# A Fourier stage whose 64x64 products become 32x32 after one more round of sums on GpSimd

## The chip, the cores and the metric

One core of one Trainium2 chip runs the program. The metric is device time in microseconds (us) of one execution. Engines are called as in the profile: PE is TensorE, DVE VectorE, ACT ScalarE, POOL GpSimd, SP the engine that issues most DMAs.

## The reference

The inputs are 8 batches of 3008 rows by 256 channels. Each batch is transformed along its rows, mixed over channels in the frequency domain, clipped softly, transformed back, and put through a wide layer with a cosine.

```
X = rfft(x, axis=1)                      # 3008 = 64 * 47 rows
Yr = Xr @ w_r - Xi @ w_i + b_r
Yi = Xr @ w_i + Xi @ w_r + b_i
Y  = sign(Y) * max(|Y| - 0.01, 0)        # for Yr and Yi
y  = irfft(Yr + 1j * Yi, axis=1)         # 24064 rows of 256 in all
h  = y @ w_in                            # 256 -> 2048
out = (h * cos(h)) @ w_out               # 2048 -> 256
```

## The kernel before, in words

The row index is split into 64 times 47 (padded to 48). Stage A takes the 64-point transform, stage B the 47-point one (`forward`), the mixing (`combine`, `wmix`), the folding (`fold`) and the inverse 47-point transform (`spread`, matmuls into `pi`); stage C takes the inverse 64-point transform (into `pc`) and turns the result for the wide layer. The wide layer runs in steps, 16 steps for each of 6 column tiles of a batch, so 96 steps a batch: `moe_step` multiplies by `win` into `ph`, makes the cosine product `u` on ACT and DVE, rounds it to `gh` on ACT, and takes the rest `gl = u - gh`. `gl` is made on POOL for the even steps (`POOL_GL = (0, 2)`) and on DVE for the odd ones. `second` multiplies `gh` and `gl` by `wout` into `po`, three steps later (`SKEW = 3`).

The Fourier work of batch b+1 is written between the wide layer's steps of batch b by generators that give back costs (`pull`, `share`), and a scheduler fixes from that the order of instructions on each engine. Each engine then runs its own list strictly in order. On POOL the list mixes `gl` with the tile sums of stage A, the sums of `combine` (`both`, `Xl`), the folding (`st`, `odd`), and the issue of DMAs (`xt`, `fq`). So a late `gl` holds PE at the line of `second` that reads it, and whatever stands ahead of `gl` in POOL's list makes it late.

Stage A of batches 2 to 7 handles six tiles a batch, two at a time: three groups a batch, 18 in all. `load` issues the DMA of a tile `xt` (512 KB) from POOL's queue; two tiles are in flight. `fold` adds and subtracts the two mirrored halves on POOL (line 460 writes `xe`, line 461 overwrites part of `xt`). `burst_of` then lets PE multiply both tiles: eight products of 64x64 with 512 columns each (a product shows as two rows of the trace). A burst is issued as one piece where its inputs allow it. ACT copies the four PSUM banks out (line 499), SP stores them to `scr1`, and the loads of the tiles two further on are issued. The sums of a group follow its loads, and its burst comes some 40 us later. After a batch's third group the next batch's first two tiles are loaded and summed.

Of the kernel before, what the change touches and what calls it, by code (L numbers as in the profile page):

```python
# [86 lines left out]


def _constants():
    n1, s = np.arange(64), np.arange(32)  # L90
    ang = 2 * np.pi * (np.outer(n1, s) % 64) / 64
# [25 lines left out]
    for sl in range(1, 32):  # L117
        for k2 in range(47):
            sig[sl, k2] = 1 if crt[sl, k2] <= N // 2 else -1
# [61 lines left out]
def tile_body(ctx: ExitStack, tc, x, w_r, w_i, b_r, b_i, w_in, w_out,  # L181
# [26 lines left out]
    def load_constants():  # L208
        with nc.allow_non_contiguous_dma(reason="bias"):
            for r, bsrc in enumerate((b_r, b_i)):  # L210
                nc.gpsimd.dma_start(bb[:, r, :], bsrc.rearrange("(c p) -> p c", p=128))
        ws["sig"] = pool["pro"].tile([96, 32], F32, name="sig", bufs=1)
        nc.gpsimd.dma_start(ws["sig"], c_sig)
        nc.gpsimd.dma_start(fi[0], c_if)
        ws["minus"] = wk.tile([128, 64], F32, tag="xe", name="minus", bufs=2)
        nc.gpsimd.tensor_scalar(out=ws["minus"], in0=ff[:, 256:], scalar1=-1.0, scalar2=None, op0=ALU.mult)
# [169 lines left out]
    def stage_out(name):  # L386
        return wk.tile([128, 1024], F32, tag="ao", name=name, bufs=3)
# [52 lines left out]
    def stage_a(b):  # L440
        scr1[b] = dr.tile([2, 24, 32, 2, 256], F32, tag="scr1", name=f"scr1_{b}")
        ld, ev = {}, {}

        def load(c):
            if c < 6:
# [4 lines left out]
                if b == 2 and c < 2:  # L450
                    behind(ins, mark["pc"].ins, "first tile")

        def fold(c):
            with floor() if b == 2 else ExitStack():
                sums(c)

        def sums(c):
            ev[c] = wk.tile([128, 2, 256], F32, tag="xe", name="xe", bufs=2)
            lo, hi = ld[c][:, :, 0], ld[c][:, :, 1]
            nc.gpsimd.tensor_tensor(out=ev[c], in0=lo, in1=hi, op=ALU.add)  # L460
            nc.gpsimd.tensor_tensor(out=lo, in0=lo, in1=hi, op=ALU.subtract)

        def store(c, ao, after=None):
            for v in range(2):
                ins = nc.sync.dma_start(
                    scr1[b][v, 4 * c:4 * c + 4].rearrange("i s r d -> (s r) i d"),
                    ao[64 * v:64 * v + 64].rearrange("p (i d) -> p i d", i=4))
                if after is not None:
                    behind(ins, after.ins, "first tile")
# [7 lines left out]
        def burst_of(cs, banks=None, home=stage_out):  # L477
# [3 lines left out]
            p = {(c, h): ps2[2 * (c - cs[0]) + h] for c in cs for h in range(2)}  # L481
            if b == 1:
                ins = burst(1 if odd else 2, [((p[c, h][64 * v:64 * v + 64], (ws["minus"] if v * g else ff[:, 256:])[64 * h:64 * h + 64],
                            ld[c][64 * h:64 * h + 64, :, g]),
                           dict(start=g == 0, stop=g == 1, skip_group_check=True))
                          for c in cs for g in range(2) for h in range(2) for v in (1, 0)])
                if pro:
                    mark["fill"] = mark["pa"] = ins
            else:
                burst(len(ps2), [((p[c, h][64 * v:64 * v + 64], ff[64 * h:64 * h + 64, 256:320],  # L490
                                   (ld[c][64 * h:64 * h + 64, :, 0] if v else ev[c][64 * h:64 * h + 64])),
                                  dict(start=True, stop=True, skip_group_check=True))
                                 for c in cs for h in range(2) for v in (1, 0)])
            if banks:
                yield 0.0
            for c in cs:
# [9 lines left out]
                else:  # L506
                    store(c, ao)
                if b > 1:
                    del ld[c], ev[c]
                    load(c + 2)  # L510
            yield BURST

        def folds(j):
            for c in (2 * j, 2 * j + 1):
                fold(c)
                yield 0.5
# [14 lines left out]
        def begin():  # L531
            load(0)
            load(1)

        return SimpleNamespace(begin=begin, folds=folds, alone=alone, release=release, one=lambda *a: burst_of([a[0]], *a[1:]),
                               group=lambda j: burst_of([2 * j, 2 * j + 1]))


    def stage_b(b):
# [15 lines left out]
        def load(q):  # L555
            if b and q < 4:
# [4 lines left out]
                for h in range(4):  # L561
                    own = q == 0 and SLOT0[h] != SLOTS[h]
                    r0 = 64 * (h // 2) + 24 * (h % 2)
                    for (v, r), s0, s1 in ((SLOT0[h], 0, 1), (SLOTS[h], 1, 8)) if own else ((SLOTS[h], 0, 8),):
                        ins = nc.sync.dma_start(t[r0:r0 + 24, 256 * s0:256 * s1].rearrange("j (s d) -> j s d", d=256),
                                                scr1[b][v, :, 8 * q + s0:8 * q + s1, r])
                        loads.append(ins)
# [462 lines left out]
    COST = 4 * (6 * GROUP + 2 * TURN + 11.0 + MIXED + QUIET + 3 * READ + BURST + QUIET + 3 * READ + BURST)  # L1030
    A_COST = 3 * (1.0 + QUIET + 3 * READ + BURST)
    HEAD = 3 * (READ + BURST) + START + BT_WAIT + FIRST
# [98 lines left out]
```

## Time and profile before

| what | value |
|---|---|
| median of 3 runs | 2578.68 us (2576.16 to 2579.6) |
| the profiled execution, its own time | 2579.13 us |
| its span | 2577.1 us |
| PE busy | 2549.1 us, 99% of the span |
| DVE, ACT, POOL busy | 72%, 65%, 40% |
| mean granted clock of TensorE | 0.998 |

The span is from the first to the last instruction; about 2.0 us lie around it. A busy share is an average over stages; PE's 99% says that PE is hardly ever idle, and where it is idle must be read from the order in time.

### The profile page before, as it was taken

What the parts mean: (1) busy time and instruction counts of PE and PEld (TensorE: products, weight loads), DVE (VectorE), ACT (ScalarE), POOL (GpSimd) and SP (SyncE); (2) the same over time, 40 slices, a digit from 0 to 9 for tenths busy, and PEclk for the clock granted to TensorE, in tenths of its full rate; (3) what the DMA queues carried; (4) which work ended last, traced back from release to release, by engine and by line L of the source; (5) the groups of instructions that cost most, each with busy time, mean ns of one, the idle gap of its engine ahead of it and who ended that gap; (6) DMA issues with size and microseconds to landing.
All of it is one profiled execution on the core that took longest, in us unless ns stands there. A gap on an engine that the chain in (4) does not pass through costs nothing.

```text
span 2577.1 us, 42991 instructions
## 1 busy us (share of the span) xinstructions
PE 2549.1 (99%) x15961; PEld 2063.7 (80%) x15961; DVE 1850.8 (72%) x2909; ACT 1679.6 (65%) x3119; POOL 1026.6 (40%) x1002
## 2 busy tenths in 40 slices
PE   9999999999999999999999999999999999999999
PEld 7577777877788777887788777887788888888888
DVE  5887766777667776777767777677776777766665
ACT  5766666666666666666666666666676666666666
POOL 2135552555334453345623545245442444222222
PEclk9999999999999999999999999999999999999999
DMA  7545444444334443254423544345433244210000
GB/s 238 188 115 148 134 116 118 112 130 139 111 82 126 136 132 98 82 154 142 130 83 98 155 131 119 91 101 144 132 104 104 85 116 114 62 45 17 17 25 16
DMA packets 172954, 283.12 MB, mean 110 GB/s; under 512 B 15608, under 2 KB 114200, under 8 KB 169160
## 3 DMA queue, kind: packets, MB, share of 16 engines
q1 hardware_dynamic: 161896, 243.78, 33.6%
q0 software_dynamic: 10112, 35.53, 4.4%
q8 instruction: 126, 2.06, 0.3%
q10 hardware_dynamic: 736, 1.05, 0.1%
q14 instruction: 84, 0.69, 0.1%
HBM read 149.76 MB, written 130.55 MB: 109 GB/s over the span
## 4 chain that ended last, share of the span: by engine, by line
PE 85%; DVE 5%; DMA 3%; ACT 2%; issue 2%; POOL 2%; SPq 0%; ACTq 0%; DVEq 0%; POOLq 0%
PE ph L936 12%; PE po L918 12%; PE po L922 12%; PE ph L937 12%; PE ph L938 12%; PE po L919 12%; PE pw L676 2%; PE pw L678 2%; PE pw L677 2%; PE pc L383 1%; PE pb L383 1%; DVE u L950 1%; DMA xt<-in_dram 1%; DVE u L947 1%; PE pw L672 1%
## 5 line engine op out<-in xcount | busy, mean ns | idle before, releaser
L331 POOL TENSOR_TENSOR gl<-u,gh 128x512 fp32r<-128x512 f32 (+1 forms) x384 | 494.0, 1286 | 1079.9 <-ACT gh L951 913.9
L949 ACT ACTIVATE u<-u 128x512 f32<-128x512 f32 (+1 forms) x768 | 478.4, 623 | 348.0 <-DVE u L947 346.9
L947 DVE SCALAR_TENSOR_TENSOR u<-ph,u 128x512 f32<-128x512 f32 (+1 forms) x768 | 515.9, 673 | 258.4 <-ACT u L946 256.5
L950 DVE TENSOR_TENSOR u<-ph,u 128x512 f32<-128x512 f32 (+1 forms) x768 | 518.5, 676 | 252.7 <-ACT u L949 240.5
L946 ACT ACTIVATE u<-ph 128x512 int32<-128x512 f32 (+1 forms) x768 | 449.9, 587 | 256.1 <-PE ph L938 248.0
L918 PE MATMUL po<-gh,wout 128*128 128x512 f32 (+1 forms) x1536 | 598.9, 390 | 4.4 <-ACT gh L951 4.4
L936 PE MATMUL ph<-xTh,win 128*128 128x512 f32 (+1 forms) x1536 | 601.5, 392 | 0.2
L951 ACT CAST gh<-u 128x512 fp32r<-128x512 f32 (+1 forms) x768 | 467.6, 610 | 202.3 <-DVE u L950 198.3
L937 PE MATMUL ph<-xTl,win 128*128 128x512 f32 (+1 forms) x1536 | 594.5, 387 | 0.0
L938 PE MATMUL ph<-xTh,win 128*128 128x512 f32 (+1 forms) x1536 | 594.0, 387 | 0.0
L919 PE MATMUL po<-gh,wout 128*128 128x512 f32 (+1 forms) x1536 | 593.6, 386 | 0.0
L922 PE MATMUL po<-gl,wout 128*128 128x512 f32 (+1 forms) x1536 | 477.8, 388 | 5.2 <-POOL gl L331 5.2
L334 DVE TENSOR_TENSOR gl<-u,gh 128x512 fp32r<-128x512 f32 (+1 forms) x384 | 304.6, 793 | 76.1 <-ACT gh L951 68.1
L936 PEld LDWEIGHTS ph<-xTh,win 128*128 128x128 f32 x1536 | 288.5, 188 | 87.5 <-issue 19.0
L922 PEld LDWEIGHTS po<-gl,wout 128*128 128x128 f32 x1536 | 287.2, 188 | 71.9 <-POOL gl L331 9.6
L918 PEld LDWEIGHTS po<-gh,wout 128*128 128x128 f32 x1536 | 288.6, 188 | 66.1 <-ACT gh L951 7.6
L938 PEld LDWEIGHTS ph<-xTh,win 128*128 128x128 f32 x1536 | 288.8, 188 | 56.3
L919 PEld LDWEIGHTS po<-gh,wout 128*128 128x128 f32 x1536 | 288.8, 188 | 51.1 <-issue 0.4
L937 PEld LDWEIGHTS ph<-xTl,win 128*128 128x128 f32 x1536 | 288.8, 188 | 51.0
L676 PE MATMUL pw<-Xh,wf 128*128 128x384 f32 x336 | 114.3, 340 | 2.9 <-ACT Xh L613 2.9
L716 POOL TENSOR_TENSOR odd<-st 128x184 f32<-128x184 f32 (+1 forms) x112 | 66.7, 595 | 122.0 <-DVE st L693 119.4
L677 PE MATMUL pw<-Xh,wf 128*128 128x384 f32 x336 | 113.4, 338 | 0.0
(119 smaller groups left out, 2443.6 us busy)
## 6 DMA issues: line engine op xcount, KB each, us to landing
scrF<-at SPq DMA_DIRECT2D x28, 1024.0 KB
z<-scrF SPq DMA_DIRECT2D x112, 256.0 KB
scrT<-tr SPq DMA_DIRECT2D x56, 512.0 KB
y<-scrT SPq DMA_DIRECT2D x112, 256.0 KB
bt<-scr SPq DMA_DIRECT2D x94, 256.0 KB
scr<-bo SPq DMA_DIRECT2D x224, 96.0 KB
scr<-ao SPq DMA_DIRECT2D x80, 256.0 KB
out_dram<-ob SPq DMA_DIRECT2D x80, 256.0 KB
```

What stands on the lines that cost most here:

```text
L331: return nc.gpsimd.tensor_tensor(out=lo, in0=x, in1=hi.bitcast(F32), op=ALU.subtract)
L918: mm(po[e][:, :n], wo[0][:, 0, f, es], gh[:, :n], start=f == 0, stop=False)
L919: mm(po[e][:, :n], wo[0][:, 1, f, es], gh[:, :n], start=False, stop=False)
L922: mm(po[e][:, :n], wo[0][:, 0, f, es], gl[:, :n], start=False, stop=f == NFC - 1)
L936: mm(h, win[:, 0, c, fs], th[:, c, :n], start=c == 0, stop=False)
L937: mm(h, win[:, 0, c, fs], tl[:, c, :n], start=False, stop=False)
L938: ins = mm(h, win[:, 1, c, fs], th[:, c, :n], start=False, stop=c == 1)
L946: nc.scalar.activation(k[:, :n], h, AF.Identity, bias=0.25, scale=1.0 / TWO_PI)
L947: nc.vector.scalar_tensor_tensor(out=u[:, :n], in0=h, scalar=1.0 / TWO_PI, in1=k[:, :n], op0=ALU.mult, op1=ALU.subtract)
L949: nc.scalar.activation(u[:, :n], u[:, :n], AF.Sin, bias=HALF_PI, scale=TWO_PI)
L950: product = nc.vector.tensor_tensor(out=u[:, :n], in0=h, in1=u[:, :n], op=ALU.mult)
L951: step = [nc.scalar.copy(gh[:, :n], u[:, :n])]
```

## The change

For batches 2 to 7, POOL makes two rounds of sums instead of one. `halve` first adds and subtracts rows n and n+32 of a tile, which the host has laid side by side, into `xe` (now one buffer of twice the size). `fold` then adds and subtracts the mirrored halves from `xe` back into `xt`. The sums of rows need the even frequencies only, the differences the odd ones, so `octet` multiplies two tiles by sixteen products of 32x32, on sixteen parts of the array, in place of eight of 64x64. The outputs lie ordered by parity, and the constants, `scr1` and the loads from it follow that order. POOL has four sums for a tile where it had two (72 more in all); the number of bytes, of DMAs and of copies out of PSUM stays.

```
+        def halve(c):
+            with floor() if b == 2 else ExitStack():
+                t = wk.tile([128, 2, 2, 256], F32, tag="xe", name="xe", bufs=1)
+                ev[c] = t
+                one, two = ld[c][:, :, 0], ld[c][:, :, 1]
+                nc.gpsimd.tensor_tensor(out=t[:, 0], in0=one, in1=two, op=ALU.add)
+                nc.gpsimd.tensor_tensor(out=t[:, 1], in0=one, in1=two, op=ALU.subtract)
+
         def fold(c):
             with floor() if b == 2 else ExitStack():
-                sums(c)
-
-        def sums(c):
-            ev[c] = wk.tile([128, 2, 256], F32, tag="xe", name="xe", bufs=2)
-            lo, hi = ld[c][:, :, 0], ld[c][:, :, 1]
-            nc.gpsimd.tensor_tensor(out=ev[c], in0=lo, in1=hi, op=ALU.add)
-            nc.gpsimd.tensor_tensor(out=lo, in0=lo, in1=hi, op=ALU.subtract)
+                t = ev.pop(c)
+                for v, op in ((0, ALU.add), (1, ALU.subtract)):
+                    nc.gpsimd.tensor_tensor(out=ld[c][:, v], in0=t[:, :, 0], in1=t[:, :, 1], op=op)
...
-                burst(len(ps2), [((p[c, h][64 * v:64 * v + 64], ff[64 * h:64 * h + 64, 256:320],
-                                   (ld[c][64 * h:64 * h + 64, :, 0] if v else ev[c][64 * h:64 * h + 64])),
-                                  dict(start=True, stop=True, skip_group_check=True))
-                                 for c in cs for h in range(2) for v in (1, 0)])
...
+        def octet(j):
+            cs = (2 * j, 2 * j + 1)
+            p = some("pa", 4)
+            burst(4, [((p[k][64 * c + 32 * w:64 * c + 32 * w + 32],
+                        ff[32 * k:32 * k + 32, 256 + 32 * w:288 + 32 * w],
+                        ld[cs[c]][32 * k:32 * k + 32, :, w]),
+                       dict(start=True, stop=True, skip_group_check=True))
+                      for c in range(2) for w in range(2) for k in range(4)])
+            for h in range(2):
+                ao = stage_out("ao")
+                for i in range(2):
+                    drained(p[2 * h + i], nc.scalar.copy(ao[:, 512 * i:512 * i + 512], p[2 * h + i]))
+                    if h == 0 or i == 0:
+                        yield Hold(READ)
+                for c in range(2):
+                    n = 4 * cs[c] + 2 * h
+                    nc.sync.dma_start(
+                        scr1[b][n:n + 2].rearrange("j v s r d -> (s r) (j v) d"),
+                        ao[64 * c:64 * c + 64].rearrange("p (x d) -> p x d", x=4))
+                del ld[cs[h]]
+                load(cs[h] + 2)
             yield BURST
 
         def folds(j):
             for c in (2 * j, 2 * j + 1):
+                halve(c)
+                yield 0.5
                 fold(c)
                 yield 0.5
...
-    A_COST = 3 * (1.0 + QUIET + 3 * READ + BURST)
+    A_COST = 3 * (2.0 + QUIET + 3 * READ + BURST)
```

The order on POOL after the first burst of batch 5 (the place of [rows 6]), before; `gl` is the wide layer's rest, `DMA xt` the load of a tile, `xe` and `xt` its sums, `sgn` and `odd` belong to the folding:

```order
L331 TENSOR_TENSOR gl<-u,gh 128x512
L448 DMA xt<-in_dram 128x1024
L460 TENSOR_TENSOR xe<-xt 128x512
L461 TENSOR_TENSOR xt<-xt 128x2x256
L460 TENSOR_TENSOR xe<-xt 128x512
L461 TENSOR_TENSOR xt<-xt 128x2x256
L706 TENSOR_TENSOR st<-st,sgn 128x8x48
L716 TENSOR_TENSOR odd<-st 128x8x23
L331 TENSOR_TENSOR gl<-u,gh 128x512 x2
```

The same place now:

```order
L336 TENSOR_TENSOR gl<-u,gh 128x512 x2
L453 DMA xt<-in_dram 128x1024 x2
L463 TENSOR_TENSOR xe<-xt 128x512
L464 TENSOR_TENSOR xe<-xt 128x512
L731 TENSOR_TENSOR st<-st,sgn 128x8x48
L470 TENSOR_TENSOR xt<-xe 128x512 x2
L741 TENSOR_TENSOR odd<-st 128x8x23
L463 TENSOR_TENSOR xe<-xt 128x512
L464 TENSOR_TENSOR xe<-xt 128x512
L336 TENSOR_TENSOR gl<-u,gh 128x512
L470 TENSOR_TENSOR xt<-xe 128x512 x2
L741 TENSOR_TENSOR odd<-st 128x8x23
```

Before the second `gl` of the place (the one that stands behind `odd` before) there are now six sums in place of four, and both loads are issued behind the first `gl`, where one of them stood ahead of it. It is the same behind the second group of a batch. Behind the third group, four sums stand ahead of that `gl` before and now.

On PE, the first group of batch 2, before (one piece):

```order
L919 MATMUL po_2331<-gh,wout 128x512
L373 MATMUL pa<-xt,ff 64x512
L383 MATMUL pa<-xe,ff 64x512
L383 MATMUL pa<-xt,ff 64x512
L383 MATMUL pa<-xe,ff 64x512
L383 MATMUL pa<-xt,ff 64x512
L383 MATMUL pa<-xe,ff 64x512
L383 MATMUL pa<-xt,ff 64x512
L383 MATMUL pa<-xe,ff 64x512
L922 MATMUL po_2330<-gl,wout 128x512
```

And now, the last rows of the group, whose first eight products stand 20 rows further up:

```order
L947 MATMUL po_2330<-gl,wout 128x512
L947 MATMUL po_2331<-gl,wout 128x512
L943 MATMUL po_2330<-gh,wout 128x512
L944 MATMUL po_2330<-gh,wout 128x512
L943 MATMUL po_2331<-gh,wout 128x512
L944 MATMUL po_2331<-gh,wout 128x512
L947 MATMUL po_2330<-gl,wout 128x512
L947 MATMUL po_2331<-gl,wout 128x512
L388 MATMUL pa<-xt,ff 32x512 x8
```

The burst stands in two halves of eight products there, and so do the other two of batch 2; before, only the third of them was in two. The 15 bursts of batches 3 to 7 are whole before and now.

## Rows read from the trace of the kernel before

**Rows 1.** The page: span, and busy time of each engine

```profile
span 2577.1 us, 42991 instructions
PE 2549.1 (99%) x15961; PEld 2063.7 (80%) x15961; DVE 1850.8 (72%) x2909; ACT 1679.6 (65%) x3119; POOL 1026.6 (40%) x1002
```

**Rows 2.** Timeline of PE: stage A's second burst of batch 5, and what follows (start, us, ...)

```profile
1218.70 0.64 PE L373 MATMUL pa<-xt,ff 64*64 64x512 f32 x1
...
1220.58 0.50 PE L922 MATMUL po<-gl,wout 128*128 128x512 f32 x1
```

**Rows 3.** Timeline of PE: a burst of sixteen 24x32 products, and what follows

```profile
1230.30 0.61 PE L373 MATMUL pi<-y,iw 24*32 24x512 f32 x1
...
1231.37 0.50 PE L936 MATMUL ph<-xTh,win 128*128 128x512 f32 x1
```

**Rows 4.** Timeline of PE: half a burst of stage A in batch 2, and what follows

```profile
357.34 0.64 PE L373 MATMUL pa<-xt,ff 64*64 64x512 f32 x1
...
358.36 0.50 PE L918 MATMUL po<-gh,wout 128*128 128x512 f32 x1
```

**Rows 5.** Groups by line: the same rest on POOL and on DVE (busy us, mean ns)

```profile
L331 POOL TENSOR_TENSOR gl<-u,gh 128x512 fp32r<-128x512 f32 (+1 forms) x384 | 494.0, 1286 | 1079.9 <-ACT gh L951 913.9 <-issue 87.7 <-PE ph L938 37.3
...
L334 DVE TENSOR_TENSOR gl<-u,gh 128x512 fp32r<-128x512 f32 (+1 forms) x384 | 304.6, 793 | 76.1 <-ACT gh L951 68.1 <-PE ph L938 0.7 <-PE po L922 0.7
```

**Rows 6.** Timeline of POOL behind the first burst of batch 5 (idle before, releaser)

```profile
1157.68 0.55 POOL L448 DMA_DIRECT2D xt<-in_dram  x1 [3.84 <-PE pa L383]
1158.58 1.29 POOL L331 TENSOR_TENSOR gl<-u,gh 128x512 fp32r<-128x512 f32 x1 [0.34 <-ACT gh L951]
...
1162.79 1.29 POOL L460 TENSOR_TENSOR xe<-xt 128x512 f32<-128x512 f32 x1 [2.40 <-DMA xt<-in_dram]
1164.16 1.50 POOL L461 TENSOR_TENSOR xt<-xt 128x512 f32<-128x512 f32 x1
...
1168.78 0.92 POOL L706 TENSOR_TENSOR st<-st,sgn 128x384 f32<-128x384 f32 x1
1169.78 0.59 POOL L716 TENSOR_TENSOR odd<-st 128x184 f32<-128x184 f32 x1
1170.33 1.30 POOL L331 TENSOR_TENSOR gl<-u,gh 128x512 fp32r<-128x512 f32 x1
```

**Rows 7.** Timeline of PE: where it reads the gl that ends rows 6

```profile
1174.91 0.62 PE L922 MATMUL po<-gl,wout 128*128 128x512 f32 x2
```

**Rows 8.** Timeline of POOL: the gl that ends the same work behind the second burst

```profile
1232.47 1.30 POOL L331 TENSOR_TENSOR gl<-u,gh 128x512 fp32r<-128x512 f32 x1
```

**Rows 9.** Timeline of PE: where it reads the gl that ends rows 8

```profile
1236.48 0.61 PE L922 MATMUL po<-gl,wout 128*128 128x512 f32 x2
```

**Rows 10.** Timeline of POOL behind the third burst of batch 5

```profile
1274.23 1.12 POOL L448 DMA_DIRECT2D xt<-in_dram  x2
1278.70 1.29 POOL L460 TENSOR_TENSOR xe<-xt 128x512 f32<-128x512 f32 x1 [3.35 <-DMA xt<-in_dram]
```

**Rows 11.** Timeline of PE: waits for gl behind the third bursts of batches 3 to 6

```profile
659.28 0.73 PE L922 MATMUL po<-gl,wout 128*128 128x512 f32 x2 [1.77 <-POOL gl L331]
...
974.49 0.73 PE L922 MATMUL po<-gl,wout 128*128 128x512 f32 x2 [1.73 <-POOL gl L331]
...
1286.79 0.50 PE L922 MATMUL po<-gl,wout 128*128 128x512 f32 x1 [0.76 <-POOL gl L331]
...
1600.60 0.72 PE L922 MATMUL po<-gl,wout 128*128 128x512 f32 x2 [0.50 <-POOL gl L331]
```

**Rows 12.** Windows behind the first two of these waits (length, PE busy, granted clock, DMA)

```profile
659.80:664.30 4.50, 4.50 (x14) 0.62 0.59 145
...
974.50:979.00 4.50, 4.50 (x20) 1.00 0.53 123
```

**Rows 13.** Timeline of POOL, two sums in a row in batch 2

```profile
231.19 2.54 POOL L460 TENSOR_TENSOR xe<-xt 128x512 f32<-128x512 f32 x2
```

**Rows 14.** Timeline of PE: the longest wait while batch 2 is prepared

```profile
394.07 0.75 PE L373 MATMUL pi<-y,iw 24*32 24x512 f32 x1 [3.63 <-DMA y<-scrT]
```

More of the change, by code (lines that the diff above doesn't have):

```diff
@@ L86, in _mirrored, with _order @@
     return np.concatenate([i, 47 - i], 2)
+def _order():
+    return np.arange(32).reshape(16, 2).T.reshape(-1)
 def _constants():
-    n1, s = np.arange(64), np.arange(32)
+    n1, s = np.arange(64), _order()
     ang = 2 * np.pi * (np.outer(n1, s) % 64) / 64
@@ L118, in _constants @@
         for k2 in range(47):
-            sig[sl, k2] = 1 if crt[sl, k2] <= N // 2 else -1
+            sig[sl, k2] = 1 if crt[s[sl], k2] <= N // 2 else -1
         f2[sl, 0, :47, 0, :47] = C
@@ L214, in load_constants @@
         nc.gpsimd.dma_start(fi[0], c_if)
-        ws["minus"] = wk.tile([128, 64], F32, tag="xe", name="minus", bufs=2)
+        ws["minus"] = wk.tile([128, 64], F32, tag="xe", name="minus", bufs=1)
         nc.gpsimd.tensor_scalar(out=ws["minus"], in0=ff[:, 256:], scalar1=-1.0, scalar2=None, op0=ALU.mult)
@@ L440, in stage_a @@
     def stage_a(b):
-        scr1[b] = dr.tile([2, 24, 32, 2, 256], F32, tag="scr1", name=f"scr1_{b}")
+        scr1[b] = dr.tile([24, 2, 32, 2, 256], F32, tag="scr1", name=f"scr1_{b}")
         ld, ev = {}, {}
@@ L465, in store @@
                 ins = nc.sync.dma_start(
-                    scr1[b][v, 4 * c:4 * c + 4].rearrange("i s r d -> (s r) i d"),
+                    scr1[b][4 * c:4 * c + 4, v].rearrange("i s r d -> (s r) i d"),
                     ao[64 * v:64 * v + 64].rearrange("p (i d) -> p i d", i=4))
@@ L481, in burst_of @@
             p = {(c, h): ps2[2 * (c - cs[0]) + h] for c in cs for h in range(2)}
[L482 to L489, printed above, removed]
-                burst(len(ps2), [((p[c, h][64 * v:64 * v + 64], ff[64 * h:64 * h + 64, 256:320],
-                                   (ld[c][64 * h:64 * h + 64, :, 0] if v else ev[c][64 * h:64 * h + 64])),
-                                  dict(start=True, stop=True, skip_group_check=True))
-                                 for c in cs for h in range(2) for v in (1, 0)])
+            ins = burst(1 if odd else 2, [((p[c, h][64 * v:64 * v + 64], (ws["minus"] if v * g else ff[:, 256:])[64 * h:64 * h + 64],
+                        ld[c][64 * h:64 * h + 64, :, g]),
+                       dict(start=g == 0, stop=g == 1, skip_group_check=True))
+                      for c in cs for g in range(2) for h in range(2) for v in (1, 0)])
+            if pro:
+                mark["fill"] = mark["pa"] = ins
             if banks:
@@ L507, in burst_of @@
                     store(c, ao)
-                if b > 1:
-                    del ld[c], ev[c]
-                    load(c + 2)
+            yield BURST
+        def octet(j):
[19 more added lines that the diff above has]
+                load(cs[h] + 2)
             yield BURST
@@ L535, in stage_a @@
         return SimpleNamespace(begin=begin, folds=folds, alone=alone, release=release, one=lambda *a: burst_of([a[0]], *a[1:]),
-                               group=lambda j: burst_of([2 * j, 2 * j + 1]))
+                               group=octet)
     def stage_b(b):
@@ L565, in load @@
                         ins = nc.sync.dma_start(t[r0:r0 + 24, 256 * s0:256 * s1].rearrange("j (s d) -> j s d", d=256),
-                                                scr1[b][v, :, 8 * q + s0:8 * q + s1, r])
+                                                scr1[b][:, v, 8 * q + s0:8 * q + s1, r])
                         loads.append(ins)
@@ L1112 @@
     xp = np.ascontiguousarray(xp).reshape(NB, 128, 24 * D)
+    pairs = xp[2:].reshape(NB - 2, 2, 64, 6, 2, 2, D)
+    rows = (np.arange(32)[:, None] + 32 * np.arange(2)) % 64
+    parted = [pairs[:, :, :, :, i][:, :, (rows + 32 * i) % 64].transpose(0, 1, 2, 4, 5, 3, 6) for i in range(2)]
+    xp[2:] = np.stack(parted, 2).reshape(NB - 2, 128, 24 * D)
     consts = _constants()
```

## The prediction

> **What bounds the kernel now.** I read the page first, for the busy shares: PE works for 2549.1 of 2577.1 us [rows 1], so the time is PE's, and a change counts by what it takes from PE's own work and by the waits that it adds there. Next the order in time on PE at stage A's bursts, for their price. Then POOL's order in time behind each burst, since POOL is the engine that gets more work: the reader is to see there how long the sums stand ahead of the next `gl`, and in PE's rows how much later that `gl` is read. Last, all waits of PE for `gl`.
>
> A burst of stage A holds PE for 1220.58 - 1218.70 = 1.88 us [rows 2]. POOL is busy for 40% only, yet PE already waits for it: behind each third burst of batches 3 to 6 the `gl` that follows the sums comes too late, by 1.77, 1.73, 0.76 and 0.50 us, 4.76 us together [rows 11]. So POOL's share of 40% does not say that there is room: at the places where the new sums go, POOL is the last or nearly the last to end.
>
> **What the change removes.** The trace of before has a burst of the new form: the sixteen products of 24x32 into `pi`, also with 512 columns, in the same four row strips and four column strips. It holds PE for 1231.37 - 1230.30 = 1.07 us [rows 3]. Eight more rows in a strip add no columns, so I price the new burst at 1.07. Bounds are 0.94, half of the old burst, and 1.88, if the strips did not overlap. Batches 3 to 7 have 15 whole bursts: 15 x (1.88 - 1.07) = 12.15 us less.
>
> In batch 2 the order shows the bursts cut in two, each half with eight products. Half an old burst, also eight products on the array, took 358.36 - 357.34 = 1.02 us [rows 4]. By that, batch 2's bursts go from 2 x 1.88 + 2 x 1.02 = 5.80 to 6 x 1.02 = 6.12 us; at best a half costs half of 1.07, 3.2 us in all. Neither counts: PE then stands 3.63 us for the landing of `y` [rows 14], which comes out of the folding on POOL. What counts there is whether `y` gets later. Its last sums stand behind up to two more sums of stage A, 0 to 2.54 us [rows 13]; I take 0.8, since the folding itself waits for DVE there.
>
> **What the change adds.** 72 sums at 2.54 / 2 = 1.27 us [rows 13] are 91 us more on POOL. They cost nothing for stage A itself: a group's sums end near 1170 [rows 6] and its burst begins at 1218.70 [rows 2]. If that cover were gone, 5 us a group would come in. They cost where a `gl` is queued behind them, because `second` on PE is queued behind that `gl`, and all of PE behind `second`.
>
> First bursts of batches 3 to 7. Before, one load went out at 1157.68, the first sum began 5.11 us later, and the `gl` behind the four sums, the sign product and `odd` ended at 1170.33 + 1.30 = 1171.63 [rows 6]. PE read it at 1174.91 [rows 7], so 3.28 us were to spare. Now both loads go out behind the `gl` that ends at 1158.58 + 1.29 = 1159.87. From there the first sum takes 4.47 us, as where two loads are issued together [rows 10], or 5.11. Then stand two sums 2.54, the sign product 0.92, two sums 2.54, `odd` 0.59, two sums 2.54 and the `gl` 1.30: 10.43 us. Where DVE works beside them a sum takes 1.50 in place of 1.29 [rows 6]; three such add 0.6. The `gl` ends between 1174.8 and 1176.0. PE comes 0.81 sooner, at 1174.1. So PE waits 0.7 to 1.9 us where it did not wait; I take the middle, 1.3, five times: 6.5.
>
> Second bursts. Here the spare was 1236.48 - (1232.47 + 1.30) = 2.71 us [rows 8, 9]. The order of PE now puts seven products of the wide layer ahead of the burst (1.6 us) and 1.1 us of stage C's small products ahead of the reading; with the shorter burst PE reads this `gl` 1.3 us sooner. The `gl` itself gets 3.2 to 4.4 us later by the same chain, less up to 1.4 because the `gl` ahead of the loads belongs to a step that now stands earlier. That leaves a wait of 0.4 to 3.0; I take 1.4, nearer to the low end, as the earlier step should hold for most of it: 7.0 for five.
>
> Third bursts. Four sums stand ahead of the `gl` now as before, but they are two independent pairs. From the first sum to PE's reading it was 1286.79 - 1278.70 = 8.09 [rows 10, 11]; now 5.08 + 0.92 + 1.30 = 7.3, with DVE beside it 7.9. PE comes 0.81 sooner. Each of the four waits grows by 0 to 0.6, I take 1.4 for all.
>
> The clock. After the wait of 1.77 us the granted clock was 0.62 over 4.5 us, a mean of the two levels 1.2 and 2.4 GHz; after one of 1.73 it stayed at 1.00 [rows 12]. The fall cost (1 - 0.62) x 4.5 = 1.7 us. With ten more waits of this size I count one more fall, 1.7 (none to five).
>
> **The sum.** -12.15 + 6.5 + 7.0 + 1.4 + 0.8 + 1.7 = +5.25 us on the profiled execution's 2579.13, so 2584.4. The median of the runs stands 0.45 below that execution, which makes 2583.9. The change then moves 12 us of PE's work into waits for POOL and gives a little back on top. About 5.2 us, 0.2%, can be told from no change, and the sum lies on that edge.
>
> The same rest takes 1286 ns on POOL and 793 on DVE [rows 5]. The Trainium skill speaks against the change here: GPSIMD Engine Reference, Engine selection, sends elementwise sums of two tiles to VectorE, because GpSimd is about half as fast at them. The trace agrees, with a ratio of 1.6. Were the added sums on DVE by that rule, none would stand ahead of `gl` on POOL, and the sum would be about -12 us; where they stand, by the rows, it is +5.
>
> **Rivals.** *POOL keeps up* (0.21). If the chain behind the loads is some 1.3 us shorter than I make it, the new waits vanish and only the third bursts' 1.4 stays: 2578.7 - 12.15 + 1.4 = 2568. For it: the spare of 3.28 and 2.71 us is more than the two sums that are added ahead of `gl`. Against it: the loads go out 2.2 us later, and PE comes sooner.
>
> *The waits feed the slow clock* (0.15). At waits of 2.0 us each PE passes the longest of the four old ones, after one of which the clock fell; with five falls the sum is -12.15 + 20 + 8.5 + 1.4 + 0.8 = +18.6, so 2597. It decides once the mean wait passes 1.8 us. For it: every wait comes on top of a burst whose products leave PE free sooner. Against it: one fall in four waits so far.
>
> *The sixteen parts don't work at once* (0.03). With 1.88 a burst nothing is gained and the waits stay: 2578.7 + 13.5 + 2 = 2594. The burst into `pi` speaks against it.
>
> **How the numbers follow.** My forecast, new waits of 0.5 to 2 us at ten places, has 0.58 and its own range of 2577 to 2592; I put 0.30 of it within 0.2% and 0.28 above. 0.03 is left for a small gain within 0.2%. So faster is 0.21, same 0.30 + 0.03 = 0.33, slower 0.28 + 0.15 + 0.03 = 0.46. The range of 2567 to 2594 takes in the first rival and the lower end of the second; the bounds of all terms together (2572 to 2604) are not met at once.
>
> **What would show it.** The burst from its first product to the next other product: 1.07 right, above 1.2 wrong. POOL behind a first burst: from the end of the `gl` ahead of the loads to the first sum 4.5 to 5.1 us, from there to the end of the next `gl` 10.4 to 11.0. Waits of PE for POOL's `gl` at the line of `second`: some 14 of 0.5 to 2 us in batches 3 to 7, about 18 to 20 us in all with the old ones; 5 us or less would make the forecast wrong on the side of the first rival, and 30 on that of the second. Other waits of PE should stay as they are; a wait of the burst itself for `xt`, or of the copies out of PSUM, is in none of the cases.

## The result, and the profile after

The changed kernel takes 2596.5 us (median; 2596.3 to 2601.4) where the kernel before, beside it, takes 2577.4: a ratio of 1.0079 (95% interval 1.0061 to 1.0096), 19 us slower. The two profiled spans differ by 17.5 us. The prediction had +5.2 us, with a range of 2567 to 2594.

The page of after: PE has less work, POOL 95 us more [rows 1].

```profile
span 2594.6 us, 43657 instructions
PE 2546.0 (98%) x16249; PEld 2064.7 (80%) x16249; DVE 1860.4 (72%) x2909; ACT 1679.7 (65%) x3119; POOL 1121.3 (43%) x1074
```

PE's order in time at the first burst of batch 5, and the `gl` product of the step that waits behind it [rows 2, 7]. The columns are start, duration, engine, line, operation; in brackets the idle time before it and what ended it.

```profile
1169.94 0.61 PE L378 MATMUL pa<-xt,ff 32*32 32x512 f32 x1
1170.40 0.68 PE L388 MATMUL pa<-xt,ff 32*32 32x512 f32 x15
1171.01 0.50 PE L961 MATMUL ph<-xTh,win 128*128 128x512 f32 x1
...
1189.16 0.73 PE L947 MATMUL po<-gl,wout 128*128 128x512 f32 x2 [1.21 <-POOL gl L336]
```

The burst holds PE for 1171.01 - 1169.94 = 1.07 us, and so do all fifteen whole bursts. POOL's order in time behind the same burst [rows 6]:

```profile
1172.19 1.29 POOL L336 TENSOR_TENSOR gl<-u,gh 128x512 fp32r<-128x512 f32 x1 [3.69 <-ACT gh L976]
1173.43 1.09 POOL L453 DMA_DIRECT2D xt<-in_dram  x2
1178.43 1.30 POOL L463 TENSOR_TENSOR xe<-xt 128x512 f32<-128x512 f32 x1 [3.92 <-DMA xt<-in_dram]
...
1181.82 3.00 POOL L470 TENSOR_TENSOR xt<-xe 128x512 f32<-128x512 f32 x2
...
1186.56 1.32 POOL L464 TENSOR_TENSOR xe<-xt 128x512 f32<-128x512 f32 x1
1187.82 1.29 POOL L336 TENSOR_TENSOR gl<-u,gh 128x512 fp32r<-128x512 f32 x1
```

From the end of the `gl` ahead of the loads (1173.48) to the first sum are 4.95 us, from there to the end of the next `gl` (1189.11) 10.7: what the prediction laid down. Of the 4.95 POOL stands idle for 3.92, because the first sum waits for the tile to land and the `gl` is queued behind it. PE's waits as a table (us in total, times, longest):

```profile
PE po L947 <- POOL gl L336: 24.3, 19, 2.5
PE po L943 <- ACT gh L976: 7.8, 8, 2.7
PE pi L378 <- DMA y<-scrT: 3.7, 1, 3.7
```

In the order in time, the waits for `gl` of batches 3 to 7 [rows 11] are 7.4 us behind first bursts (1.2 to 2.1 each), 9.3 behind second ones (1.3 to 2.5) and 4.6 behind third ones (0.3 to 1.7). After the wait of 2.46 us that ends at 622.35 the granted clock was 0.58 from 624 to 628, a mean of the levels 1.2 and 2.4 GHz [rows 12], and 1.00 in the next 4 us:

```profile
622.00:624.00 2.00, 1.65 (x66) 1.28 (x66) 1.30 (x3) 1.50 (x3) 2.00 (x3) 0.98 0.74 210
624.00:628.00 4.00, 4.00 (x23) 3.30 (x16) 3.21 (x5) 2.19 (x4) 2.01 (x2) 0.58 0.51 152
628.00:632.00 4.00, 4.00 (x19) 3.34 (x19) 3.15 (x7) 3.13 (x6) 1.39 (x2) 1.00 0.33 120
```

**Where the time went.** The wide layer's 768 steps are the same in all kernels, so I take from each trace the start of a step's last `gl` product and subtract that of before. Step 0 ends the opening; batch 2's bursts lie between steps 36 and 72 (248 to 376 us); between 72 and 98 follow the first sums of batch 3 and the wait for `y`; then batches 3 to 7. After is behind by 1.84 us at step 0, 4.08 at step 36, 12.32 at step 72, **13.95 at step 98** and 17.50 at the last. So batches 3 to 7 add 3.55 from there, near the forecast (-12.15 + 6.5 + 7.0 + 1.4 + 1.7 = +4.45). What the prediction lacks lies ahead of step 98, where it had 0.8. The times up to a step are those of one profiled execution of each kernel.

### The profile page after: what moved, and what is told of

It reads as the page before. It is cut to its first block, busy times and chain, and to the rows that moved or that the text cites. A ratio compares the mean times of both kernels' runs of the same rounds, so it can differ in the third digit from the quotient of the medians.

```text
span 2594.6 us, 43657 instructions
## 1 busy us (share of the span) xinstructions
PE 2546.0 (98%) x16249; PEld 2064.7 (80%) x16249; DVE 1860.4 (72%) x2909; ACT 1679.7 (65%) x3119; POOL 1121.3 (43%) x1074
## 4 chain that ended last, share of the span: by engine, by line
PE 79%; POOL 8%; DVE 4%; DMA 4%; ACT 3%; issue 2%; SPq 0%; ACTq 0%; DVEq 0%; POOLq 0%
PE ph L961 11%; PE po L947 11%; PE ph L962 11%; PE ph L963 11%; PE po L943 11%; PE po L944 11%; DMA xt<-in_dram 3%; POOL gl L336 2%; PE pw L703 2%; PE pw L701 2%; PE pw L702 2%; POOL xt L470 2%; POOL xe L464 2%; PE pc L388 1%; POOL xe L463 1%
## 5 line engine op out<-in xcount | busy, mean ns | idle before, releaser
L339 DVE TENSOR_TENSOR gl<-u,gh 128x512 fp32r<-128x512 f32 (+1 forms) x384 | 312.5, 814 | 84.7 <-ACT gh L976 78.8
L961 PEld LDWEIGHTS ph<-xTh,win 128*128 128x128 f32 x1536 | 289.6, 189 | 88.7 <-issue 19.9
L703 PE MATMUL pw<-Xl,wf 128*128 128x384 f32 x336 | 113.1, 339 | 0.0
```

The costliest lines, as they stand in the source:

```text
L961: mm(h, win[:, 0, c, fs], th[:, c, :n], start=c == 0, stop=False)
```

## The experiments

The same readings for every run. "old" and "new" are the products and sums of batches 3 to 7; "old sums" are the two a tile of before, "new sums" the four of after. The last columns are us behind before at the start of a step's last `gl` product ("last" is step 767). `floor()` is the program's hold on the scheduler: what stands inside it may not be placed ahead of the last wide-layer step but one before the place where the program gives it out.

| run | edit | median us | ratio (95%) | step 0 | 36 | 98 | last |
|---|---|---|---|---|---|---|---|
| after | new | 2596.5 | 1.0079 (1.0061-1.0096) | 1.8 | 4.1 | 14.0 | 17.5 |
| e1 | new, batch 2 old | 2583.1 | 1.0028 (1.0017-1.0040) | 0.3 | 0.3 | 1.3 | 2.9 |
| e8 | new, old pace in batch 2 | 2596.8 | 1.0081 (1.0066-1.0096) | 0.6 | 0.6 | 14.1 | 17.8 |
| e3 | new products, no sums | 2555.8 | 0.9923 (0.9909-0.9938) | 1.6 | 3.9 | -0.9 | -21.9 |
| e6 | old products, sums of new | 2606.5 | 1.0120 (1.0105-1.0135) | 0.7 | 0.7 | 12.3 | 23.1 |
| e2 | new, no floor | 2603.9 | 1.0106 (1.0091-1.0121) | 7.4 | 11.2 | 21.9 | 24.7 |
| e4 | new, `halve` on DVE | 2653.8 | 1.0298 (1.0283-1.0313) | 0.1 | 2.4 | 13.5 | 75.9 |
| e9 | new, all sums on DVE | 2650.4 | 1.0285 (1.0270-1.0301) | 1.0 | 3.3 | 11.6 | 72.8 |
| e10 | new, all `gl` on DVE | 2600.2 | 1.0093 (1.0077-1.0110) | 0.8 | 8.1 | 14.9 | 20.0 |
| e11 | new, floor in all batches | 2613.6 | 1.0143 (1.0127-1.0158) | 0.7 | 3.0 | 10.5 | 35.9 |
| e12 | e11, sums given out earlier | 2591.4 | 1.0057 (1.0042-1.0072) | 4.8 | 7.2 | 5.3 | 14.5 |
| e14 | e12, batch 2 old | 2585.9 | 1.0037 (1.0024-1.0050) | 1.9 | 2.1 | -1.9 | 7.7 |
| e15 | old, sums placed as in e14 | 2569.8 | 0.9974 (0.9964-0.9984) | 1.7 | 1.7 | -0.7 | -5.3 |
| e16 | e14, sums one by one | 2595.6 | 1.0070 (1.0055-1.0085) | 1.1 | 0.9 | -1.9 | 17.0 |
| e17 | e16, batch 2 new | 2600.6 | 1.0088 (1.0072-1.0105) | 2.3 | 5.6 | 4.5 | 23.1 |
| e18 | old, sums placed as in e16 | 2565.5 | 0.9954 (0.9939-0.9968) | 1.0 | 0.9 | -3.0 | -13.9 |
| e19 | e16, still earlier | 2592.1 | 1.0058 (1.0043-1.0073) | 0.9 | 0.8 | -1.6 | 14.2 |
| e20 | old, sums placed as in e19 | 2573.1 | 0.9986 (0.9977-0.9996) | 0.4 | 0.4 | -3.6 | -6.9 |
| e21 | new, batch 2's sums earlier | 2594.0 | 1.0068 (1.0050-1.0087) | 0.3 | 2.6 | 9.2 | 13.8 |

### Is it batch 2, and is it the sums?

My theory was that batch 2's added sums on POOL make the loss; the rivals were the opening, and the faster pace of the plan (`A_COST` and the yields doubled).

e1 gives batch 2 its own old sums, products and pace (the main lines of the edit):

```diff
-                halve(c)
-                yield 0.5
-                fold(c)
-                yield 0.5
+                if b == 2:
+                    sums(c)          # as before
+                    yield 0.5
+                else: ...            # as after
-        group=octet
+        group=(lambda j: burst_of([2 * j, 2 * j + 1])) if b == 2 else octet
```

> The changed kernel, with batch 2 alone put back: its four sums a group, its 64x64 products and its pace in the plan are those of before, so its instructions up to the end of batch 2's preparation stand in the order of before. Theory A (the loss that I did not foresee sits in batch 2; batches 3 to 7 lose 3.6 us net): the last product of the wide layer's step 98 comes within 2 us of before (the changed kernel: 14.0 later), the end some 3 to 6 us later than before, 2581 to 2583, and 12 to 15 below the changed kernel. Rival (the loss is the opening or a drift between runs, not batch 2): step 98 still 10 us late or more, about 2594.

e8 keeps the new batch 2 and takes the pace of before for it:

```diff
-                yield 0.5
+                yield 0.5 if b > 2 else 0.25
-        (A_COST if b + 2 < NB else 0.0)
+        (A_COST - (0.0 if b else 3.0) if b + 2 < NB else 0.0)
```

> The changed kernel with its sums and octets in batch 2 as well, but the plan's pace of before while batch 2 is prepared: each of the two pairs of sums counts 0.25 there, and the share of batch 0 is worked out with 1.0 a group in place of 2.0. Theory S (the sums of batch 2 themselves make gh and gl late on POOL): no better than the changed kernel by more than 3 us, 2593 to 2597, with step 98 still 10 us or more behind before. Rival P (the faster pace, which pulls batch 2's products forward and so moves everything around them, makes the loss): step 98 within 5 us of before, 2584 to 2588.

e3 keeps the products and drops the sums, so that its output is not the reference's:

```diff
-                halve(c)
-                yield 0.5
-                fold(c)
-                yield 0.5
+                yield 1.0
```

> The changed kernel without any of the sums of batches 2 to 7: the sixteen products read the tiles as they land, and the pace stays that of the changed kernel. It leaves out the folding, so that its output is not the reference's; its time is that of the shorter bursts alone. Theory S (POOL's sums make all of the loss): bursts of 1.07 us, no wait for POOL's gl over 1 us in batches 3 to 7, step 98 within 3 us of before, the end 2560 to 2566 (2577.4 - 12.15 for the bursts - 4.8 for the old waits behind the third bursts, +0 to 3 in batch 2). Rival P (batch 2's loss comes from the pace): the same in batches 3 to 7, but step 98 some 10 us late, the end 2570 to 2576.

e6 is before, with two sums more for each tile:

```diff
+            nc.gpsimd.tensor_tensor(out=ev[c], in0=lo, in1=hi, op=ALU.subtract)
+            nc.gpsimd.tensor_tensor(out=ev[c], in0=lo, in1=hi, op=ALU.subtract)
             nc.gpsimd.tensor_tensor(out=ev[c], in0=lo, in1=hi, op=ALU.add)
```

> The kernel before, with two more sums for each tile on POOL in batches 2 to 7 (their result is written over by the third), its 64x64 bursts and its pace as they were: the new load of POOL alone. Theory S: in batches 3 to 7 PE waits for gl behind first and second bursts, each wait some 0.8 us shorter than in the changed kernel since PE comes 0.81 later: 3.4 + 5.2 + about 4 in place of 4.8, so +8 us; and batch 2 loses 10 to 12 as in the changed kernel: about 2596. Rival P (batch 2 loses by the pace): batch 2 within 3 us of before, about 2585.

The four agree. With batch 2 put back, step 98 is 1.3 us late, not 14; without sums it is early; with the sums alone and the old products it is 12.3 late. The pace costs 2.3 us by step 36 (every kernel with the new pace in batch 2 shows it or more: 0.7 to 3.0 in e11, 0.3 to 2.6 in e21; e1, e6, e8 don't), yet e8 ends where after does. So the added sums cost 10 to 14 us from step 36 to 98, whatever the pace. e3, which came out below its range, also shows what the shorter bursts are worth without any sums: 21.0 us in batches 3 to 7, of which 12.15 are the bursts, 4.8 the old waits for `gl`, 1.7 the clock fall behind one of them; two waits of 1.35 for `Xh` that before had are gone as well. e6's median came out 10 us above the expectation. Its profiled execution, at 2602.5 the fastest of its four, adds 10.9 us in batches 3 to 7 where 8 were expected; what the slower ones add is in no trace.

### Is it floor(), or the engine?

e2 drops `floor()` from `halve` and `fold`:

```diff
-            with floor() if b == 2 else ExitStack():
+            with ExitStack():
```

> The changed kernel without floor() around halve and fold: in batch 2, too, POOL's sums may go as soon as their tiles have landed, as in batches 3 to 7. Theory F (it is the tie to a step close ahead of the burst that makes batch 2 dear): step 98 within 4 us of before (14.0 in the changed kernel), the end 2584 to 2588. Rival L (it is the amount of POOL's work in that stretch, 24 more sums of 1.27 us beside the folding that ends in y, wherever they stand): step 98 still 9 us late or more, 2592 to 2598.

F fell: from step 36 to 98 e2 loses 10.7 us, as after with 9.9. It is no clean test of the tie, though, since without it the sums go to the other end, right behind their loads, and PE waits 3.38 and 3.16 us (at 270 and 398) for a `gl` behind them. Four of them even stand ahead of the first `gl`, for which PE waits 4.95 us at 127; that is most of the 7.4 us by which its opening is late.

e4 gives `halve` to DVE; e9 does the same in `fold`; e10 leaves the sums and gives DVE every `gl`:

```diff
-                nc.gpsimd.tensor_tensor(out=t[:, 0], in0=one, in1=two, op=ALU.add)
-                nc.gpsimd.tensor_tensor(out=t[:, 1], in0=one, in1=two, op=ALU.subtract)
+                nc.vector.tensor_tensor(out=t[:, 0], in0=one, in1=two, op=ALU.add)
+                nc.vector.tensor_tensor(out=t[:, 1], in0=one, in1=two, op=ALU.subtract)
```

```diff
-POOL_GL = (0, 2)
+POOL_GL = ()
```

> The changed kernel with the added first sums (halve) on DVE in all of batches 2 to 7; fold stays on POOL, which then has the load of before, and DVE gets 72 sums, at the 793 ns of its gl some 57 us. Theory S (POOL's queue is all that the added sums hurt): no wait for gl behind first and second bursts, step 98 within 3 us of before, 2562 to 2568. Rival D (DVE is as tight: the two operations on the way to gh stand behind the sums, and PE waits for u or gh in place of gl): waits of PE for DVE or ACT of some 15 us, 2575 to 2590.

> The changed kernel with all sums of stage A on DVE, the old ones too: 144 of them, some 115 us at 793 ns, and POOL has 91 us less to do than before. Theory S: the waits for gl behind all three bursts of a batch are gone, as in the run without sums, and the time is within 6 us of that run, 2556 to 2562. Rival D (DVE's sums make gh late): four sums in a row are 3.2 us on DVE, and two groups of waits of 1 to 2 us a burst give 2570 to 2585.

> The changed kernel with every gl on DVE: POOL keeps all sums, but no gl stands behind them; DVE gets 384 more operations of 793 ns, 305 us, and goes from 72 to about 84% of the span. Theory S: the waits for POOL's gl vanish, only those of the bursts for xt and of y are left, 2560 to 2570. Rival D: DVE has the two operations of 0.67 us and a gl of 0.79 in each step of 3.2 us, and at the folding some 1.2 us more; it falls behind there, PE waits for gh and gl from DVE, 2580 to 2610.

Both runs with sums on DVE are 74 to 77 us slower than before, far beyond what either theory said. DVE's order in time in e4, and PE's first wait behind it:

```profile
543.71 0.69 DVE L972 SCALAR_TENSOR_TENSOR u<-ph,u 128x512 f32<-128x512 f32 x1 [3.13 <-ACT u L971]
547.54 0.69 DVE L463 TENSOR_TENSOR xe<-xt 128x512 f32<-128x512 f32 x1 [3.15 <-DMA xt<-in_dram]
548.15 0.68 DVE L464 TENSOR_TENSOR xe<-xt 128x512 f32<-128x512 f32 x1
548.76 0.68 DVE L975 TENSOR_TENSOR u<-ph,u 128x512 f32<-128x512 f32 x1
```

```profile
556.33 0.79 PE L961 MATMUL ph<-xTh,win 128*128 128x512 f32 x1 [4.45 <-DVE u L975]
```

A sum takes 0.69 us on DVE, not 1.29. But the first sum stands in DVE's list before its tile has landed, and the 3.15 us idle in front of it hold back `u`, which every step needs (15 such idles, 45.8 us in e4). PE then has waits of 2 to 5 us for `u`, and behind them the granted clock falls: its mean over the span is 0.984, in after 0.996, which over 2653 us is 32 us of PE's full speed. So the rows put the loss on DVE down to the landing; a run with sums on DVE behind their landing, which would show it, was not made. In e10 DVE is busy for 80%, and the waits for POOL's `gl` have become 22 us of waits for `u` and 7.5 for `gh`: 2600.2 us is near the time of after and in the range of rival D.

### Is it the place of the sums?

The rows of after show POOL idle for the landing ahead of each group of batches 3 to 7, though the burst is some 50 us away. e11 holds `halve` and `fold` in all batches, so that the sums go where the program has them. e12 also moves the line that gives them out:

```diff
-            with floor() if b == 2 else ExitStack():
+            with floor():
```

```diff
+            if q and more:
+                yield from a.folds(q - 1)
             mix = on.wmix(q)
             yield from take(mix, 2)
 ...
-            if q and more:
-                yield from a.folds(q - 1)
```

e14 is e12 with batch 2 old, e15 the control, before with the same two edits for batches 3 to 7.

> The changed kernel with floor() around halve and fold in all batches, not in batch 2 alone. In the changed kernel POOL's first sum of a group in batches 3 to 7 stands right behind the two loads and idles 3.3 to 4.2 us until the tile lands, with a gl queued behind it, though its burst is 50 to 60 us away. Here the sums stand where the program has them, some 10 to 15 us ahead of the burst and long behind the landing. Theory W (the waits for gl in batches 3 to 7 are made by this idling in POOL's queue): nearly all of the 21 us of waits behind the fifteen bursts go, batch 2 stays as it is, 2574 to 2582. Rival L (POOL has too much work near a burst wherever the sums stand, as batch 2 with its floor() shows): each of the five batches loses some 5 to 10 us more, 2605 to 2640.

> As the last, and the sums of a group are also given out earlier in the program: ahead of the first two products of the mixing for the step, not between its third and fourth; in batch 2 as well. Theory W: in batches 3 to 7 as the last; in batch 2 the sums come away from the burst and from the folding that ends in y, which gives back 5 to 10 of its 10 us: 2564 to 2574. Rival L: batch 2 loses as before (POOL's work in that stretch is the same), 2574 to 2584.

> The run with batch 2 put back, and in batches 3 to 7 the sums with floor() and given out early. Theory W: batch 2 costs 1 us, and batches 3 to 7 come near the run without sums, which gained 21 us there: -12 for the bursts, -5 for the old waits, -2 for a clock fall: 2558 to 2566, faster than both kernels. Rival L: 2575 to 2585, as with batch 2 put back alone.

> The kernel before with its own sums held by floor() in all batches and given out early in batches 3 to 7: a control for the part of the gain that has nothing to do with the sixteen products. Theory W: its four waits for gl behind third bursts, 4.8 us, and the clock fall behind one of them, 1.7, go: 2568 to 2573. Rival L: 2575 to 2580.

The control gains as expected, and in e12 batch 2 loses nothing from step 36 to 98. But batches 3 to 7 lose: 25.4 us in e11 (rival L's range), 9.1 in e12 and 9.5 in e14 (above the ranges of both theories). Under 1 us of waits for POOL's `gl` is left in them, so theory W was right on the wait and wrong on the time.

Part of it is the burst itself. In e11 all fifteen bursts of batches 3 to 7 stand in two halves; PE at the first of batch 5:

```profile
1165.82 0.61 PE L378 MATMUL pa<-xt,ff 32*32 32x512 f32 x1
...
1166.83 0.50 PE L961 MATMUL ph<-xTh,win 128*128 128x512 f32 x1
...
1171.32 1.09 PE L388 MATMUL pa<-xt,ff 32*32 32x512 f32 x16
1172.34 0.50 PE L943 MATMUL po<-gh,wout 128*128 128x512 f32 x1
```

A half holds PE for 1.01 to 1.02 us, a whole new burst for 1.07, a whole old one for 1.88. So a new burst in two halves costs more than an old one: 15 x (2.03 - 1.07) = 14.4 of the 21.8 us by which e11 loses more than after in these batches. In e12, e14, e16 and e17 the third bursts run one half after the other, and hold PE for 1.7 to 2.9 us with the waits for `xt` in them; the controls' old bursts stay whole at 1.88.

In e12 and e14 PE waits over 13 us for `u`. In e14, POOL, then DVE, then PE around 895 us:

```profile
890.93 2.55 POOL L470 TENSOR_TENSOR xt<-xe 128x512 f32<-128x512 f32 x2
893.44 1.28 POOL L336 TENSOR_TENSOR gl<-u,gh 128x512 fp32r<-128x512 f32 x1
894.68 0.59 POOL L763 TENSOR_TENSOR odd<-st 128x184 f32<-128x184 f32 x1
```

```profile
890.78 0.65 DVE L996 SCALAR_TENSOR_TENSOR u<-ph,u 128x512 f32<-128x512 f32 x1
895.30 0.45 DVE L771 STREAM_TRANSPOSE tr<-odd 128x256 f32<-128x256 f32 x1 [3.87 <-POOL odd L763]
...
896.16 0.68 DVE L999 TENSOR_TENSOR u<-ph,u 128x512 f32<-128x512 f32 x1
```

```profile
901.54 0.50 PE L967 MATMUL po<-gh,wout 128*128 128x512 f32 x1 [1.15 <-ACT gh L1000]
```

`odd` stands behind the sums, DVE's transpose of it idles 3.87 us, `u` stands behind the transpose, `gh` behind `u`. I took this for the cause (H). e16 gives the sums out one by one between the products of the mixing, with batch 2 old; e17 does so in batch 2 as well; e18 is the control with the old sums. e19 and e20 give them out farther ahead. The edit of e16, in short:

```diff
             mix = on.wmix(q)
-            yield from take(mix, 2)
+            yield from some_of(one, 2)      # one = a.singly(q - 1): one sum, with floor(), a yield
+            yield from take(mix, 1)
+            yield from some_of(one, 1)
+            yield from take(mix, 1)
 ...
```

> Batch 2 put back, and in batches 3 to 7 the eight sums of a group given out one by one between the products of the mixing, each held by floor(), at the same cost in the plan: POOL gets at most two sums in a row ahead of an odd or a gl. Theory H (in the run with the sums early but in rows of four, odd stood behind the sums, DVE's transpose of it stood 33 us in all for POOL, and u and gh behind the transpose were late): the wait of DVE for odd falls to 15 to 20 us as in the control, and batches 3 to 7 gain 8 us or more in place of losing 9.5: 2562 to 2572. Rival L (it is the amount of POOL's work, in rows or singly): 2578 to 2590.

> The changed kernel with the sums one by one in batch 2 as well. Theory H: batch 2 loses 0 to 5 us, not 12, so 2564 to 2576. Rival L: batch 2 loses 9 to 14 as in the changed kernel, and the time is 2574 to 2600.

> Control: the kernel before, its own four sums a group given out one by one in batches 3 to 7. Theory H and rival L alike: as the control with early sums, 2567 to 2573, since two sums in a row were no burden there.

> Batch 2 put back; in batches 3 to 7 the sums singly as in the run before, but given out farther ahead of their burst: from the turn behind the last inverse on, between the folding of the other side and the first products of the mixing, some 20 to 45 us ahead of the burst in place of 5 to 20. Theory C (what is left of the loss is crowding: close ahead of the burst POOL also has sgn, odd and gl, and DVE's gl is stretched there): batches 3 to 7 gain, 2562 to 2574. Rival L (the amount of POOL's work costs the time wherever it stands): 2580 to 2596.

> Control: the kernel before with its own sums given out at the same places. By both theories 2563 to 2570, as the control with single sums.

H fell as the main cause: in batches 3 to 7 of e16 DVE waits 16 us in all for `odd` (e14 33, its control e15 15), but they lose 18.9 us, and 15.8 in e19, so theory C fell too. (In e17 batch 2, from step 36 to 98, gains 1.2.) Rival L, the amount of POOL's work, is not out for batches 3 to 7. The old sums at the same places gain, though e20 missed its range (2573.1, not 2563 to 2570): e18 is the fastest kernel that computes the reference, 0.46% below before. Its PE hardly waits for `gl` at all, and POOL never idles for a tile, where before it idled 48.6 us:

```profile
L949 PE MATMUL po<-gl,wout 128*128 128x512 f32 (+1 forms) x1536 | 477.0, 387 | 0.4 <-POOL gl L331 0.4
```

One thing that the eight sums do in their new places shows on DVE. In e11, DVE, then POOL:

```profile
1535.28 9.59 DVE L339 TENSOR_TENSOR gl<-u,gh 128x512 fp32r<-128x512 f32 x1
1544.79 0.68 DVE L972 SCALAR_TENSOR_TENSOR u<-ph,u 128x512 f32<-128x512 f32 x1
```

```profile
1535.36 2.55 POOL L470 TENSOR_TENSOR xt<-xe 128x512 f32<-128x512 f32 x2
1537.86 0.58 POOL L741 TENSOR_TENSOR odd<-st 128x184 f32<-128x184 f32 x1
1538.40 1.29 POOL L463 TENSOR_TENSOR xe<-xt 128x512 f32<-128x512 f32 x1
1539.66 1.28 POOL L464 TENSOR_TENSOR xe<-xt 128x512 f32<-128x512 f32 x1
1540.91 0.96 POOL L743 TENSOR_TENSOR st<-st 128x368 f32<-128x368 f32 x1
1541.84 2.47 POOL L470 TENSOR_TENSOR xt<-xe 128x512 f32<-128x512 f32 x2
```

A `gl` whose median is 0.69 us stands on DVE for 9.59, as long as POOL goes from one instruction to the next without a gap, and `u` stands behind it. e11 has two such, and PE waits 9.1 us behind them. In e16 five `gl` take 3.2 to 3.7 us, and DVE's mean `gl` goes from 793 ns [rows 5] to 854. The Trainium skill has this rule (SBUF — State Buffer, Who interferes with whom): a DVE instruction with both inputs in SBUF contends with a GpSimd instruction that reads SBUF, and the one that comes later is blocked. The trace agrees on the contention: `gl` has both inputs in SBUF and is stretched, `u`, with one input in PSUM, takes at most 0.70 in all of e11. It does not agree on the order: by these rows `gl` starts 0.08 us ahead of POOL's sum, and it is kept out through eight instructions.

e21 last, after with batch 2's sums alone given out early (`b` is here the batch before):

```diff
+            if q and more and b == 1:
+                yield from a.folds(q - 1)
             mix = on.wmix(q)
 ...
-            if q and more:
+            if q and more and b > 1:
                 yield from a.folds(q - 1)
```

> The changed kernel with one shift: the sums of batch 2 are given out ahead of the first two products of the mixing for the step, still held by floor(); batches 3 to 7 stay as in the changed kernel. Theory K (in batch 2 it was the place that cost: the sums stood right ahead of the burst and of the folding for y): step 98 stands no later against before than step 36 does (in the changed kernel 9.9 us later), batches 3 to 7 add 2 to 4 us as they do there, and the time is 2581 to 2587, 10 to 15 below the changed kernel and still above before. Rival L (24 more sums in that stretch cost some 10 us wherever they stand): 2591 to 2598.

K was right for batch 2's own sums: from step 36 to 72 e21 loses 0.7 us where after loses 8.2, so there the place made the loss. From 72 to 98 it then loses 5.9, which K did not have, and the time, 2594.0, lies in rival L's range. The rows put the 5.9 down to the first sums of batch 3, right behind their loads, without `floor()`; e12, which holds them too, gains 2.5 there. POOL, then PE:

```profile
366.26 1.12 POOL L453 DMA_DIRECT2D xt<-in_dram  x2
372.86 1.50 POOL L463 TENSOR_TENSOR xe<-xt 128x512 f32<-128x512 f32 x1 [5.48 <-DMA xt<-in_dram]
...
381.17 1.26 POOL L336 TENSOR_TENSOR gl<-u,gh 128x512 fp32r<-128x512 f32 x1
```

```profile
382.48 0.80 PE L949 MATMUL po<-gl,wout 128*128 128x512 f32 x1 [4.97 <-POOL gl L336]
```

## Why the prediction was wrong

**Right: the burst.** Sixteen products in 1.07 us, taken from the burst into `pi`; the third rival is out.

**Right: the waits behind bursts of batches 3 to 7.** First bursts 7.4 us (forecast 6.5), second 9.3 (7.0), one more clock fall (two, before one). That the sum is so near, +3.55 against +4.45, is in part luck: third bursts were to cost 1.4 more and cost 0.2 less (4.6, before 4.8), and two waits for `Xh`, 2.7 us, went that the prediction did not speak of.

**Wrong: "Neither counts. ... I take 0.8", the step on batch 2.** I held that PE's wait for `y` covers everything there and bounded 24 added sums by what they could do to `y`. From step 36 to 72 after loses 8.2 us: PE waits 1.18 and 2.74 for `gh` (at 281 and 344) and 0.98 for `gl`, where before had no wait over 0.3, and two clock falls follow, of some 1.7 each (granted clock below), 8.3 in all. From 72 to 98 another 1.6, though PE's waits there are no longer in sum than before's: 1.47 for the `gl` behind batch 3's first sums is new, but three for `gh` (2.2 in all) shrank to 0.3. The wait for `y` stayed (3.67, before 3.63) [rows 14]: it absorbs nothing that comes ahead of it, because `y` moved back with all that feeds it, from 394 to 408 us.

```profile
282.00:286.00 4.00, 3.02 (x8) 2.40 (x8) 3.26 (x6) 3.03 (x6) 2.64 (x2) 0.57 0.42 92
344.00:348.00 4.00, 4.00 (x12) 3.02 (x11) 3.15 (x7) 3.10 (x7) 3.06 (x3) 0.57 0.35 135
```

The path to the longest wait stands in the rows of DVE, ACT and PE:

```profile
330.50 0.45 DVE L749 STREAM_TRANSPOSE tr<-odd 128x256 f32<-128x256 f32 x1 [2.45 <-DMA scr<-ao]
...
333.95 1.23 ACT L974 ACTIVATE u<-u 128x512 f32<-128x512 f32 x2 [4.53 <-DVE u L972]
...
343.68 0.51 PE L943 MATMUL po<-gh,wout 128*128 128x512 f32 x1 [2.74 <-ACT gh L976]
```

The sums of the group's second tile end at 318.76, the second half of the burst follows at 319.80, and the copies and stores of `ao` behind it. The transposed tile `tr` takes a buffer of the same three as `ao`, so DVE's transpose stands 2.45 us for a store to land (before, at the same place, 0.23), and `u` and `gh` stand behind it. The same idle is 2.96 us at 264.5, ahead of the wait of 1.18. In e3, e12, e17 and e21 no such idle is left from step 36 to 72, and they lose 1.7 us at most there. It is the path in after and not the only one: in e6 batch 2's waits are others (1.66 us for `gl`, 1.62 for `xt`).

That the sums are the cause is shown by e1, e3, e6 and e8. That it is their place is shown for batch 2's own sums, up to step 72, by e21, and up to step 98 by e12 and e17, which keep all of batch 2's sums and gain 1.8 and 1.2 us there.

**Missing: the pace.** `A_COST` and the yields doubled, and I gave the plan no price. It costs 2.3 us by step 36. No sum shows it, since e8 without it loses more in batch 2.

**Not mine: the opening.** 1.84 us at step 0. Kernels whose PE, DVE, ACT and POOL have the same order there show 0.3 (e21) to 4.8 (e12), so this is an execution's or a program's chance, not the change; why is open.

**The rivals.** "POOL keeps up" is out. "The waits feed the slow clock" gave nearly the measured time, for a wrong reason: in batches 3 to 7 the clock fell twice, not five times. The -12 us that I gave to the added sums on DVE were wrong too: e4 took 77 us more than before, and e9, with all sums there, 74. The rule of the Trainium skill that I weighed there (GPSIMD Engine Reference, Engine selection: elementwise sums of two tiles belong on VectorE) holds for the price, 0.69 against 1.29 us a sum, but not for this kernel as e4 and e9 order it, where the waiting sum stands in the list of `u`.

**Open.** Why the octet's sums, given out anywhere but where after has them, cost batches 3 to 7 more than their waits for `gl` did. Rows show four ways: bursts in halves (most of it in e11), `odd` behind sums, DVE's `gl` beside POOL, sums that end after the burst is due (PE waits 0.7 us for `xt` five times in e16). In e19 the bursts are whole, and PE's waits (15 us more than before) and the slow clock (8.5 us more) make the loss. But for e11's halves the shares were not told apart, since each edit also lets the scheduler change the order of much else.

## What to carry over

A stage that waits for one thing anyway does not make work in front of it free: follow each added instruction to everything behind it in its engine's list, and from there to the next engine. An instruction that waits for a DMA holds up all that stands behind it in its list. Moving the old sums to where their tiles have landed gained 0.14 to 0.46%; the new sums, twice as many, lost by the same move in batches 3 to 7, so the landing is not all that a place is judged by: look also at whether the burst stays whole, and at what the sums hold up in their new place, here `odd` on POOL and `gl` on DVE. The new products without any sums (e3) gain 19.9 us on before, e18 gains 11.9: the two lie 8 us apart. A faster engine was no better a home for the sums while they stood in its list ahead of their landing.

## What I had not expected of the hardware

One instruction of DVE stood 9.59 us, fourteen times its usual 0.69, beside six rows of POOL's work without a gap. Moving 72 sums to the engine that does them in half the time cost 57 us against after, 77 against before. Sixteen products in two halves held PE for 2.03 us, in one piece for 1.07. And the 120 us up to step 0, in the same order on PE, DVE, ACT and POOL, differed by 4.8 us between the profiled executions of kernels.
